# Staging buffers for w3, a later pooled sum of v, and the order of work between the dense layers and the first expert

## The chip, the cores and the metric

The kernel runs on one core of one Trainium2 chip. The metric is the device time of one execution in microseconds (us). The core has five engines that run their own instruction queues in order: TensorE (PE in the profile, its weight loads PEld), VectorE (DVE), ScalarE (ACT), GpSimd (POOL) and SyncE (SP). SyncE computes nothing; it issues transfers, and a transfer that must wait there holds up all those queued behind it. Other engines can issue transfers as well.

## The reference

```
x   = attention(q, k, v)            # 4 x 8 heads, 576 positions, 64 wide; two parts added:
                                    #   pooled by 4 along the sequence (q_d, k_d, v_d = means of 4 rows), repeated 4 times
                                    #   local: |i - j| < 4
x   = ((x @ w1) * (x @ w2)) @ w3 @ w_out       # 2304 rows, 512 -> 1024 -> 1024 -> 512
e   = argmax(x @ w_gate); g = softmax weight of e; o = sigmoid(x @ w_output_gate)[e]
out = g * o * (relu(x @ e_w1[e]) @ e_w2[e])    # each row through its one of 8 experts
```

The weights of the dense layers come as 64-bit floats, and results are kept to nearly 32 bits: each large product is three matmuls, of an upper and a lower half (hi x hi, hi x lo, lo x hi).

## The kernel before

**The first 110 us: weights.** 64-bit weights are loaded as 128x512 tiles of 512 KB, turned into 32-bit floats by three VectorE instructions (lines 138 to 140, `f64_bits`) and split into halves by ScalarE and then VectorE or GpSimd. First come eight tiles of w_out (staging buffers W0 to W7), then sixteen of w3: `f64_load("3", n)` puts tile n into buffer W8 + n % 4, so tile n + 4 is loaded once tile n is converted. The loop over `i` (line 932) converts two of them, and TensorE multiplies them with w_out (`wc_half`), so that later layers use one matrix `wc`. Then w1 and w2 follow, whose halves lie in W0 to W15 as well.

**Attention** is cut into 16 units (two heads each) of five steps: `a_T` (sums of q and k, GpSimd), `a_S1` (scores, exponentials), `a_S2` (normalisation), `a_V1` (transposes), `a_V2` (product with v). They run four deep, as `side`, a few in each turn of the weight loop and later of the dense layers. A unit's v comes twice: `vw` for the local part, and `v4` (the profile's tile v) for the pooled part. `v4` has one buffer; its load is issued at the end of step `a_S1`, and two GpSimd additions at the end of `a_S2` (lines 248 and 249) sum it.

**The dense layers** go over six groups of 384 rows: `g1_step` makes hidden rows, `g2_step` multiplies 128 of them with half of `wc`, copies the result to `yb` and stores it to DRAM (`yd`, and the right half to `yh`) from SyncE. The Tile framework puts the instructions of each engine in an order of its own, by the program's order and a planned timeline, unless lines like `issue_after` fix it.

**From the last group to the first expert** the order of TensorE is written out (`ordered`, lines 997 on): the right halves of the last group, what is left of group 4, the routing (`route_pos`, `route_tok`, `route_rank`, `route_idx`), then the left halves of the last group, tiles 0, 1 and 2. `x_gather` fetches the first expert's rows from DRAM by GpSimd: first their right halves (`yh`), and, after the last left half is stored, the left ones (`yd`). `x_prep` transposes them, in three blocks. `ew_load` and `ew_split` load and split expert weights (512 KB each): (0, 0, i) are the four quarters of the first expert's first matrix, (0, 1, i) those of its second. While the left halves are on their way, TensorE does `ga_part`, the half of the first product that needs only the right halves, for six of eight column tiles f (six PSUM tiles), and `route_gtab` (three matmuls for the gate tables). `route_gates` (lines 653 to 657) makes the gates on VectorE. Then `x_prep` of the left halves, `ga_step` for f = 0 to 7, and `gb_step`, the second product, whose f = 6 and 7 need quarter (0, 1, 3). `behind(rows, load)` holds a load until the gather `rows` has landed.

Of the kernel before, what the change touches and what calls it, by code (L numbers as in the profile page):

```python
# [1 line left out]

# [6 lines left out]
F32 = mybir.dt.float32  # L9
# [4 lines left out]
I64 = mybir.dt.int64  # L14
# [6 lines left out]
P = 128  # L21
B, H, S, D = 4, 8, 576, 64
NT, DM, DF, E = 2304, 512, 1024, 8
KD, KF = DM // P, DF // P
G = 384
NG = NT // G
# [22 lines left out]
def attention_moe_kernel(ctx: ExitStack, tc: tile.TileContext, q, k, vw_in, v4_in, w1, w2, w3, w_out,  # L49
# [15 lines left out]
    def mt(shape, dt, name, tag=None, bufs=None):  # L65
        return main.tile(shape, dt, name=name, tag=tag or name, bufs=bufs)
# [52 lines left out]
    def f64_load(m, n):  # L119
        if m == "o":  # L120
            t = mt([P, 512], I64, "f64w", tag=f"W{n}")
            src = w_out[P * n:P * n + P, :]
        elif m == "3":
            t = mt([P, 512], I64, "f64w", tag=f"W{8 + n % 4}")
            src = w3[n]
        else:
            t = mt([P, 512], I64, "f64", tag=f"W{3 + 4 * m}") if n % 2 and n < 6 else mt([P, 512], I64, "f64", bufs=2)
            src = (w1, w2)[m][n]
        for c in pieces(m, n):
            f64_last[0] = nc.sync.dma_start(out=t[:, c], in_=src[:, c])  # L130
        staged[m, n] = t
# [17 lines left out]
    def at(shape, dt, name, bufs=1):  # L149
        return att.tile(shape, dt, name=name, tag=name, bufs=bufs)  # L150
# [24 lines left out]
            nc.sync.dma_start(out=kz[c, h, 3:3 + S], in_=k[u, c])  # L175

    def a_loadd(u):
        v4 = at([72, 2, 4, 2 * D], F32, "v4")
        nc.sync.dma_start(out=v4.rearrange("p k r n -> p (k r n)"), in_=v4_in[u])
        st[u]["v4"] = v4  # L180

    def a_loadv(u):
        vw = at([P, 6, 2 * D], F32, "vw")
# [50 lines left out]
    def a_S2(u):  # L234
        d = st[u]
        sm, ed = d["sm"], d["ed"]
        su = at([P, 6, 2], F32, "su", bufs=2)
        sd = d["zd"]
        nc.vector.tensor_reduce(out=su, in_=sm, axis=AX.X, op=ALU.add)
        nc.vector.tensor_scalar(su, su, 1e-9, None, op0=ALU.add)  # L240
        nc.vector.reciprocal(su, su)
        nc.gpsimd.tensor_tensor(sm, sm, su.unsqueeze(3).to_broadcast([P, 6, 2, 32]), op=ALU.mult)
        nc.vector.reciprocal(sd, sd)
        nc.gpsimd.tensor_tensor(ed, ed, sd.unsqueeze(2).to_broadcast([96, 3, 144]), op=ALU.mult)
        v4 = d["v4"]
        vd = at([72, 2, 2, D], F32, "vd", bufs=2)
        vt = v4[:, :, 0:2]
        nc.gpsimd.tensor_tensor(vt, vt, v4[:, :, 2:4], op=ALU.add)
        nc.gpsimd.tensor_tensor(vd.rearrange("p k h d -> p k (h d)"), vt[:, :, 0], vt[:, :, 1], op=ALU.add)
        d.update(vd=vd)  # L250

    def a_V1(u):
        d = st[u]
        sm, ed = d["sm"], d["ed"]
        sT = at([P, 12, 32], F32, "sT")
        nc.vector.transpose(sT, sm.rearrange("p b h k -> p (b h) k"))
        for j in range(4):
            r = slice(32 * j, 32 * j + 32)
            nc.scalar.copy(out=bd[r, :, 24 * j:24 * j + 24], in_=sT[r, :, 0:24])
        pt = at([72, 2, 288], F32, "pt")  # L260
        for kb in range(2):
            pv = psa.tile([P, 512], F32, name="at", tag="at")
            with burst():
                for qb in range(3):
                    nc.tensor.transpose(pv[0:72, 96 * qb:96 * qb + 96], ed[:, qb, 72 * kb:72 * kb + 72], ident[0:96, 0:96])  # L265
            nc.scalar.copy(out=pt[:, kb], in_=pv[0:72, 0:288])
        d["pt"] = pt
# [149 lines left out]
    def mm3(ps, whi, wlo, xhi, xlo, first, last):  # L417
        nc.tensor.matmul(ps, whi, xhi, start=first, stop=False)  # L418
        nc.tensor.matmul(ps, whi, xlo, start=False, stop=False)  # L419
        return nc.tensor.matmul(ps, wlo, xhi, start=False, stop=last)  # L420
# [34 lines left out]
    lg = {}  # L455
    yn = [0]

    def g2_step(g, t, hf):
        ps = ps2.tile([P, 512], F32, name="g2", tag="g2")
        n0, n1 = HALF[hf], HALF[hf + 1]  # L460
        for f in range(KF):
            c = slice(P * t, P * t + P)
            mm3(ps[:, 0:HN[hf]], hts[g, f][0][:, c], hts[g, f][1][:, c], wc[:, f, 0, n0:n1], wc[:, f, 1, n0:n1],
                f == 0, f == KF - 1)
        r0 = G * g + P * t
        n = DM // 2
        yn[0] += 1
        y = yb[:, yn[0] % 3, :]
        if hf == 1:
            if t == 0:  # L470
                lg[g] = mt([P, CPG, 2 * E], F32, "lg", bufs=2)
            nc.vector.tensor_copy(lg[g][:, t, :], ps[:, n:n + 2 * E])
            nc.vector.tensor_copy(y, ps[:, 0:n])
        else:
            nc.scalar.copy(out=y, in_=ps[:, 0:n])
        store = nc.sync.dma_start(out=yd[r0:r0 + P, n0:n0 + n], in_=y)
        if hf == 1:
            nc.sync.dma_start(out=yh[r0:r0 + P, :], in_=y)
        return store


    def at_psum():
        if psb is None:
            return psa.tile([P, 512], F32, name="at", tag="at")
        return psb.tile([P, 512], F32, name="tr", tag="tr", bufs=2)

    psb = None
    acc = mt([P, E], F32, "acc")
    tab = mt([P, 3, E, NC], F32, "tab")
    rt = {}  # L490
# [184 lines left out]
    def ordered(fn, *args):  # L675
        with tc.issue_after(pe[0]):
            res = fn(*args)
        pe[0] = next(i for i in reversed(nc.cur_bb.bb.instructions) if i.engine == mybir.EngineType.PE)
        return res
# [67 lines left out]
    def ga_part(r, f, k0, k1, first, last):  # L747
        C = CAPS[r]
        hi, lo = ew[r, 0, f // 2]
        if first:  # L750
            if f < 4 or last:
                gp[f] = psb.tile([P, 512], F32, name="g1", tag="g1", bufs=4)
            else:
                gp[f] = ps2.tile([P, 512], F32, name="g2", tag="g2")
        for kk in range(k0, k1):
            c = slice(256 * kk + P * (f % 2), 256 * kk + P * (f % 2) + P)
            mm3(gp[f][:, 0:C], hi[:, c], lo[:, c], xT[r][0][:, kk, 0:C], xT[r][1][:, kk, 0:C],
                first and kk == k0, last and kk == k1 - 1)
# [248 lines left out]
    early = mt([P, 3, 1024], F32, "early", tag="xr")  # L1007
    for i in range(2):
        ew_load(0, 0, i)
    ordered(g2_step, NG - 1, 0, 0)  # L1010
    rows = x_gather(0, 1)
    behind(rows, ew_load(0, 0, 2))
    behind(rows, ew_load(0, 1, 0, early[:, 0]))
    ew_split(0, 0, 0)
    ordered(g2_step, NG - 1, 1, 0)
    for b in range(NBLK[0] - 1):
        ordered(x_prep, 0, b, KD // 2, KD)
    ew_split(0, 0, 1)
    store = ordered(g2_step, NG - 1, 2, 0)
    with tc.issue_after(store.ins):  # L1020
        ew_load(0, 1, 1, early[:, 1])
    rows = x_gather(0, 0)
    behind(rows, ew_load(0, 0, 3))
    last = ordered(x_prep, 0, NBLK[0] - 1, KD // 2, KD)
    with after(last):
        ew_split(0, 0, 2)
        route_gate(NG - 1)
        rhs = mt([P, CPG, 2 * E * NC], F32R, "rhs", tag="W15")
        for c in range(CPG):
            gate_rhs(NG - 1, c, rhs[:, c])  # L1030
        ew_split(0, 1, 0)
    for f in range(6):
        ordered(ga_part, 0, f, KD // 2, KD, True, False)
    ordered(route_gtab, NG - 1, rhs)
    route_gates()
    with tc.issue_after(rows.ins):
        first = ew_split(0, 1, 1)
    for b in range(NBLK[0]):
        last = ordered(x_prep, 0, b, 0, KD // 2)
    with after(last):  # L1040
        ew_split(0, 0, 3)
    for i in range(2, 4):
        behind(rows, ew_load(0, 1, i, early[:, 2] if i == 2 else None))
    for r in range(E):
        for f in range(KF):
            last = ordered(ga_step, r, f)
            if (r, f) == (1, 0):
                with after(last):
                    overflow_tables()
            if f % 2 == 0:  # L1050
                if r > 0:
                    ew_split(r, 1, f // 2)
                elif f < 4:
                    with after(last):
                        ew_split(r, 1, 2 + f // 2)
                if r + 1 < E:
                    ew_load(r + 1, 0, f // 2)
            if f % 2 == 1 and r > 0 and f // 2 < NBLK[r - 1]:
                ordered(o_step, r - 1, f // 2)
            if f == 4 and r + 1 < E:  # L1060
                with tc.issue_after(first.ins):
                    x_gather(r + 1)
        for dc in range(KD if r + 1 < E else 0):
            ordered(gb_step, r, dc)
            with after(last):
                ew_split(r + 1, 0, dc)
            ew_load(r + 1, 1, dc)
            if dc < NBLK[r + 1]:
                ordered(x_prep, r + 1, dc)
# [64 lines left out]
```

## Time and profile before

| | |
|---|---|
| median of 3 runs | 733.2 us (728.99, 733.2, 734.5) |
| the profiled execution | 731.68 us, span 729.9 us (first to last instruction) |
| busy: TensorE, VectorE, ScalarE, GpSimd | 695.8, 422.8, 286.1, 340.7 us |
| mean granted TensorE clock | 0.992 |

The span is what the trace covers; 1.8 us of the execution lie around it. TensorE is busy for 95% of it.

### The profile page before, as it was taken

What the parts mean: (1) busy time and instruction counts of PE and PEld (TensorE: products, weight loads), DVE (VectorE), ACT (ScalarE), POOL (GpSimd) and SP (SyncE); (2) the same over time, 40 slices, a digit from 0 to 9 for tenths busy, and PEclk for the clock granted to TensorE, in tenths of its full rate; (3) what the DMA queues carried; (4) which work ended last, traced back from release to release, by engine and by line L of the source; (5) the groups of instructions that cost most, each with busy time, mean ns of one, the idle gap of its engine ahead of it and who ended that gap; (6) DMA issues with size and microseconds to landing.
All of it is one profiled execution on the core that took longest, in us unless ns stands there. A gap on an engine that the chain in (4) does not pass through costs nothing.

```text
span 729.9 us, 14702 instructions
## 1 busy us (share of the span) xinstructions
PE 695.8 (95%) x5710; PEld 666.0 (91%) x5711; DVE 422.8 (58%) x884; ACT 286.1 (39%) x664; POOL 340.7 (47%) x339
## 2 busy tenths in 40 slices
PE   5887999999999999999999999989999999999995
PEld 3677989899999999999999999979999999999994
DVE  8997889854545446253242343575776656765830
ACT  3455435563444136135212121345353444544510
POOL 6975567873562157032011020166474655765511
PEclk9999999999999999999999999999999999999998
DMA  8978546363243043111100101665454744545301
GB/s 327 265 251 250 217 124 214 108 196 119 83 126 102 30 109 97 52 40 44 37 30 1 44 1 44 207 246 180 154 175 145 257 159 162 208 169 198 116 25 42
DMA packets 38266, 97.73 MB, mean 134 GB/s; under 512 B 6019, under 2 KB 12931, under 8 KB 38193
## 3 DMA queue, kind: packets, MB, share of 16 engines
q1 hardware_dynamic: 34768, 86.82, 36.5%
q0 software_dynamic: 3424, 9.93, 3.8%
q8 instruction: 46, 0.75, 0.5%
q14 instruction: 28, 0.22, 0.1%
HBM read 84.93 MB, written 12.29 MB: 133 GB/s over the span
## 4 chain that ended last, share of the span: by engine, by line
PE 77%; issue 7%; POOL 5%; DVE 5%; DMA 3%; ACT 1%; SPq 0%; POOLq 0%; DVEq 0%; ACTq 0%
PE g L418 23%; PE g L419 22%; PE g L420 22%; PE at L281 2%; DMA v<-in_v_dram 2%; PE tr L712 1%; PE at L221 1%; PE at L277 1%; DVE cv L139 1%; PE at L209 1%; PE tr L805 1%; DVE cv L138 1%; DVE wf L140 1%; PE at L265 1%; POOL out_dram L795 1%
## 5 line engine op out<-in xcount | busy, mean ns | idle before, releaser
L418 PE MATMUL g<-xh,W 128*128 128x384 f32 x384 | 131.9, 344 | 0.9 <-ACT a L446 0.9
L420 PE MATMUL g<-xh,W 128*128 128x384 f32 x384 | 129.2, 337 | 0.8 <-POOL W L397 0.7
L419 PE MATMUL g<-xl,W 128*128 128x384 f32 x384 | 129.2, 336 | 0.0
L739 DVE TENSOR_TENSOR W<-raw,W 128x1024 fp32r<-128x1024 f32 x32 | 87.7, 2771 | 32.8 <-ACT W L737 23.6
L739 POOL TENSOR_TENSOR W<-raw,W 128x1024 fp32r<-128x1024 f32 x29 | 82.9, 2879 | 36.0 <-ACT W L737 33.0
L418 PE MATMUL g<-xT,W 128*128 128x288 f32 (+6 forms) x256 | 81.5, 318 | 1.0 <-ACT xT L716 1.0
L419 PE MATMUL g<-xT,W 128*128 128x288 f32 (+6 forms) x256 | 79.8, 312 | 0.0
L420 PE MATMUL g<-xT,W 128*128 128x288 f32 (+6 forms) x256 | 79.6, 311 | 0.0
L451 POOL TENSOR_TENSOR h<-a,h 128x384 fp32r<-128x384 f32 x30 | 30.6, 1021 | 101.6 <-ACT h L449 101.6
L418 PEld LDWEIGHTS g<-xh,W 128*128 128x128 f32 x384 | 72.1, 188 | 2.6 <-ACT a L446 1.5
L420 PEld LDWEIGHTS g<-xh,W 128*128 128x128 f32 x384 | 72.1, 188 | 1.9 <-POOL W L397 1.8
L419 PEld LDWEIGHTS g<-xl,W 128*128 128x128 f32 x384 | 72.2, 188 | 0.1
L418 PE MATMUL g<-h,W 128*128 128x288 f32 (+5 forms) x224 | 69.9, 312 | 0.0
L418 PE MATMUL g<-wc,h 128*128 128x272 f32 (+1 forms) x240 | 68.7, 287 | 0.0
L419 PE MATMUL g<-wc,h 128*128 128x272 f32 (+1 forms) x240 | 68.3, 286 | 0.0
L419 PE MATMUL g<-h,W 128*128 128x288 f32 (+5 forms) x224 | 68.0, 304 | 0.0
L420 PE MATMUL g<-h,W 128*128 128x288 f32 (+5 forms) x224 | 68.0, 303 | 0.0
L420 PE MATMUL g<-wc,h 128*128 128x272 f32 (+1 forms) x240 | 67.9, 285 | 0.0
L737 ACT CAST W<-raw 128x1024 fp32r<-128x1024 f32 x61 | 59.8, 1046 | 9.0 <-DMA raw<-in_moe_w_dram 4.9
L447 DVE TENSOR_TENSOR a<-g,a 128x384 f32<-128x384 f32 x48 | 26.6, 554 | 55.6 <-PE g L420 50.3
L765 ACT ACTIVATE h<-g 128x288 fp32r<-128x288 f32 (+6 forms) x64 | 28.0, 437 | 77.1 <-PE g L420 71.5
L795 POOL DMA_INDIRECT out_dram<-orow,b_si x24 | 23.5, 978 | 62.9 <-DVE orow L794 59.3
(257 smaller groups left out, 1702.2 us busy)
## 6 DMA issues: line engine op xcount, KB each, us to landing
raw<-in_moe_w_dram SPq DMA_DIRECT2D x61, 512.0 KB
f64w<-in_moe_w_dram SPq DMA_DIRECT2D x16, 512.0 KB
f<-in_moe_w_dram SPq DMA_DIRECT2D x16, 512.0 KB
vw<-in_vw_dram SPq DMA_DIRECT2D x16, 384.0 KB
kc<-in_k_dram SPq DMA_DIRECT2D x16, 288.0 KB
qT<-in_q_dram SPq DMA_DIRECT2D x16, 288.0 KB
kz<-in_k_dram SPq DMA_DIRECT2D x32, 144.0 KB
v<-in_v_dram SPq DMA_DIRECT2D x16, 288.0 KB
```

The source lines that it names most:

```text
L138: nc.vector.tensor_scalar(c, hi, 3, 0x3FFFFFF8, op0=ALU.logical_shift_left, op1=ALU.bitwise_and)
L139: nc.vector.scalar_tensor_tensor(c, hi, 0xC0000000, c, op0=ALU.bitwise_and, op1=ALU.bitwise_or)
L281: nc.tensor.matmul(xl[c // 3][64 * h:64 * h + 64, 96 * (c % 3):96 * (c % 3) + 96], vw[:, c, D * h:D * h + D], bd[:, 2 * c + h, :], start=T ...
L418: nc.tensor.matmul(ps, whi, xhi, start=first, stop=False)
L419: nc.tensor.matmul(ps, whi, xlo, start=False, stop=False)
L420: return nc.tensor.matmul(ps, wlo, xhi, start=False, stop=last)
L447: nc.vector.tensor_tensor(a, pp[1][:, 0:G], a, op=ALU.mult)
L451: eng.tensor_tensor(lo, a, hi.bitcast(F32), op=ALU.subtract)
L737: nc.scalar.copy(out=hi, in_=t)
L739: ins = eng.tensor_tensor(lo, t, hi.bitcast(F32), op=ALU.subtract)
L765: return nc.scalar.activation(out=t[:, 0, 0:C], in_=ps[:, 0:C], func=AF.Relu), nc.vector.scalar_tensor_tensor(t[:, 1, 0:C], ps[:, 0:C], 0. ...
L795: ins = nc.gpsimd.indirect_dma_start(out=out, out_offset=bass.IndirectOffsetOnAxis(ap=rt["si"][0:n, r, b:b + 1], axis=0), in_=t[0:n], in_o ...
```

## The change

Sixteen w3 tiles rotate through ten staging buffers in place of four (W0, W1, W2, W4, W5, W6 are those of w_out that w1 and w2 don't use for their own staging). `v4` has two buffers, and its two sums move from the end of `a_S2` to the start of `a_V1`, one step later. In the stretch before the first expert: the stores of the last three left halves are issued by ScalarE; the last block's right-half transposes stand in the middle of the last `g2_step` instead of behind it; `ga_part` does seven column tiles, the seventh in one of the two PSUM tiles of the transposes, which then have one while the flag `alone` is set; `route_gtab` moves behind column tile 1 of the first expert, and `route_gates` behind its last one; quarter (0, 0, 3) is loaded with (0, 0, 2), before the left-half gather, and split before the gate work; all four quarters (0, 1, i) are split behind `ga_step` f = 0, 2, 4 and 6, the first two of which were split earlier before, and (0, 1, 1) is loaded after the left-half gather.

```diff
-            t = mt([P, 512], I64, "f64w", tag=f"W{8 + n % 4}")
+            t = mt([P, 512], I64, "f64w", tag=f"W{(8, 9, 10, 11, 0, 1, 2, 4, 5, 6)[n % 10]}")
...
-        v4 = at([72, 2, 4, 2 * D], F32, "v4")
+        v4 = at([72, 2, 4, 2 * D], F32, "v4", bufs=2)
...
-        v4 = d["v4"]
+
+    def a_V1(u):
+        d = st[u]
+        sm, ed, v4 = d["sm"], d["ed"], d["v4"]
         vd = at([72, 2, 2, D], F32, "vd", bufs=2)
         vt = v4[:, :, 0:2]
         nc.gpsimd.tensor_tensor(vt, vt, v4[:, :, 2:4], op=ALU.add)
         nc.gpsimd.tensor_tensor(vd.rearrange("p k h d -> p k (h d)"), vt[:, :, 0], vt[:, :, 1], op=ALU.add)
...
-    def g2_step(g, t, hf):
+    def g2_step(g, t, hf, middle=None, queue=None):
...
+            with tc.issue_after(pe[0]) if middle and f > KF // 2 else nullcontext():
+                end = mm3(ps[:, 0:HN[hf]], hts[g, f][0][:, c], hts[g, f][1][:, c], wc[:, f, 0, n0:n1], wc[:, f, 1, n0:n1],
+                          f == 0, f == KF - 1)
+            if middle and f == KF // 2:
+                pe[0] = end.ins
+                middle()
...
-        store = nc.sync.dma_start(out=yd[r0:r0 + P, n0:n0 + n], in_=y)
+        store = (queue or nc.sync).dma_start(out=yd[r0:r0 + P, n0:n0 + n], in_=y)
...
-        return psb.tile([P, 512], F32, name="tr", tag="tr", bufs=2)
+        tr[0] += 1
+        tag = "tr" if alone[0] or tr[0] % 2 else "tx"
+        return psb.tile([P, 512], F32, name="tr", tag=tag, bufs=1)
...
-            if f < 4 or last:
+            if f == 6 and not last:
+                gp[f] = psb.tile([P, 512], F32, name="tr", tag="tx", bufs=1)
+            elif f < 4 or last:
...
-    ordered(g2_step, NG - 1, 0, 0)
+    ordered(g2_step, NG - 1, 0, 0, None, nc.scalar)
     rows = x_gather(0, 1)
-    behind(rows, ew_load(0, 0, 2))
+    for i in range(2, 4):
+        behind(rows, ew_load(0, 0, i))
     behind(rows, ew_load(0, 1, 0, early[:, 0]))
     ew_split(0, 0, 0)
-    ordered(g2_step, NG - 1, 1, 0)
+    ordered(g2_step, NG - 1, 1, 0, None, nc.scalar)
     for b in range(NBLK[0] - 1):
         ordered(x_prep, 0, b, KD // 2, KD)
     ew_split(0, 0, 1)
-    store = ordered(g2_step, NG - 1, 2, 0)
-    with tc.issue_after(store.ins):
-        ew_load(0, 1, 1, early[:, 1])
+    last = []
+    ordered(g2_step, NG - 1, 2, 0, lambda: last.extend(ordered(x_prep, 0, NBLK[0] - 1, KD // 2, KD)), nc.scalar)
     rows = x_gather(0, 0)
-    behind(rows, ew_load(0, 0, 3))
-    last = ordered(x_prep, 0, NBLK[0] - 1, KD // 2, KD)
     with after(last):
         ew_split(0, 0, 2)
+        ew_split(0, 0, 3)
         route_gate(NG - 1)
         rhs = mt([P, CPG, 2 * E * NC], F32R, "rhs", tag="W15")
         for c in range(CPG):
             gate_rhs(NG - 1, c, rhs[:, c])
-        ew_split(0, 1, 0)
-    for f in range(6):
+    alone[0] = True
+    for f in range(7):
         ordered(ga_part, 0, f, KD // 2, KD, True, False)
-    ordered(route_gtab, NG - 1, rhs)
-    route_gates()
-    with tc.issue_after(rows.ins):
-        first = ew_split(0, 1, 1)
     for b in range(NBLK[0]):
         last = ordered(x_prep, 0, b, 0, KD // 2)
-    with after(last):
-        ew_split(0, 0, 3)
-    for i in range(2, 4):
-        behind(rows, ew_load(0, 1, i, early[:, 2] if i == 2 else None))
+    for i in range(1, 4):
+        behind(rows, ew_load(0, 1, i, early[:, i] if i < 3 else None))
+    first = None
     for r in range(E):
         for f in range(KF):
             last = ordered(ga_step, r, f)
...
-                elif f < 4:
+                else:
                     with after(last):
-                        ew_split(r, 1, 2 + f // 2)
+                        split_ = ew_split(r, 1, f // 2)
+                        first = split_ if f == 2 else first
                 if r + 1 < E:
                     ew_load(r + 1, 0, f // 2)
+            if r == 0 and f == 1:
+                ordered(route_gtab, NG - 1, rhs)
+            if r == 0 and f == KF - 1:
+                alone[0] = False
+                with after(last):
+                    route_gates()
```

## Rows read from the trace of the kernel before

**Rows 1.** The page: busy us of each engine, share of the span, instructions.
```profile
PE 695.8 (95%) x5710; PEld 666.0 (91%) x5711; DVE 422.8 (58%) x884; ACT 286.1 (39%) x664; POOL 340.7 (47%) x339
```
**Rows 2.** Windows: length, busy us by engine (instructions), granted clock, DMA share, GB/s.
```profile
20.00:30.00 10.00, 8.12 (x103) 6.02 (x100) 8.56 (x17) 6.03 (x20) 9.68 (x15) 1.00 1.01 305
30.00:40.00 10.00, 8.47 (x104) 7.50 (x104) 9.97 (x24) 3.44 (x12) 8.18 (x11) 1.00 0.80 231
20.00:69.00 49.00, 40.26 (x511) 35.41 (x508) 43.49 (x91) 25.47 (x84) 37.23 (x51) 1.00 0.87 260
```
**Rows 3.** TensorE's waits, 20 to 150 us: total us, times, longest.
```profile
PE g L418 <- DVE wc L383: 6.5, 4, 3.9
PE at L209 <- DMA kz<-in_k_dram: 1.4, 1, 1.4
```
**Rows 4.** Timelines of SP, POOL, ACT, PE, 53 to 70 us: start, us, instruction, [idle before].
```profile
53.12 0.33 SPq L168 DMA_DIRECT2D kc<-in_k_dram  x1
...
60.19 1.28 POOL L248 TENSOR_TENSOR v<-v 72x512 f32<-72x512 f32 x1 [4.04 <-DMA v<-in_v_dram]
63.41 0.67 POOL L197 TENSOR_TENSOR kc<-kc 128x288 f32<-128x288 f32 x1 [1.07 <-DMA kc<-in_k_dram]
...
65.43 0.52 ACT L227 ACTIVATE sm<-sm 128x384 f32<-128x384 f32 x1 [4.23 <-POOL sm L215]
69.18 0.40 PE L418 MATMUL g<-wo,w3T 128*128 128x272 f32 x1 [3.89 <-DVE wc L383]
```
**Rows 5.** SyncE's waits, 20 to 90 us: total us, times, longest.
```profile
SPq L130 <- DVE wf L140: 10.3, 8, 3.6
SPq L179 <- POOL vd L249: 6.9, 5, 2.3
```
**Rows 6.** GpSimd and TensorE, 92 to 95 us: the last v sum of the stage.
```profile
92.27 1.31 POOL L248 TENSOR_TENSOR v<-v 72x512 f32<-72x512 f32 x1 [2.79 <-DMA v<-in_v_dram]
94.86 0.39 PE L420 MATMUL g<-wo,w3T 128*128 128x256 f32 x1 [0.96 <-POOL w3T L371]
```
**Rows 7.** Window over the first of two stretches of lower clock.
```profile
70.35:73.76 3.41, 3.41 (x17) 3.40 (x16) 1.84 (x4) 1.23 (x4) 2.44 (x4) 0.50 0.59 167
```
**Rows 8.** Timelines of PE, ACT, SP and POOL, 467 to 483 us; window of `ga_part`.
```profile
467.58 0.35 SPq L725 DMA_DIRECT2D raw<-in_moe_w_dram  x1
470.39 0.33 PE L712 MATMUL tr<-ident,xr 96*128 96x96 f32 x2
471.03 0.33 SPq L476 DMA_DIRECT2D yd<-yb  x1
475.19 0.96 POOL L694 DMA_INDIRECT xr<-yd,b_g  x1 [10.21 <-DVE r_gs L574]
476.45 0.95 POOL L694 DMA_INDIRECT xr<-yd,b_g  x1 [0.30 <-issue]
477.37 0.86 PE L599 MATMUL tr<-rhs,rb 128*128 128x288 f32 x3
477.71 0.92 POOL L694 DMA_INDIRECT xr<-yd,b_g  x1 [0.30 <-issue]
479.32 0.41 PE L712 MATMUL tr<-ident,xr 128*128 128x128 f32 x2 [0.85 <-DMA xr<-yd,b_g]
481.57 0.38 PE L712 MATMUL tr<-ident,xr 96*128 96x96 f32 x2 [1.84 <-DVE xT L716]
482.36 0.42 PE L418 MATMUL g<-xT,W 128*128 128x352 f32 x1 [0.41 <-ACT xT L716]
...
471.28:477.37 6.09, 6.09 (x36) 5.88 (x37) 5.29 (x18) 3.37 (x5) 1.88 (x2) 1.00 0.59 195
```
**Rows 9.** Timelines of GpSimd and VectorE, 478 to 482 us.
```profile
478.65 2.35 POOL L739 TENSOR_TENSOR W<-early,W 128x1024 fp32r<-128x1024 f32 x1
478.77 2.41 DVE L655 TENSOR_TENSOR b_gt<-tab 128x144 f32<-128x144 f32 x1
```
**Rows 10.** The page's groups of instructions: ScalarE's casts of expert weights.
```profile
L737 ACT CAST W<-raw 128x1024 fp32r<-128x1024 f32 x61 | 59.8, 1046 | 9.0 <-DMA raw<-in_moe_w_dram 4.9
```

More of the change, by code (lines that the diff above doesn't have):

```diff
@@ L1 @@
-from contextlib import ExitStack, contextmanager
+from contextlib import ExitStack, contextmanager, nullcontext
 import concourse.bass as bass
@@ L177, in a_loadd @@
     def a_loadd(u):
-        v4 = at([72, 2, 4, 2 * D], F32, "v4")
+        v4 = at([72, 2, 4, 2 * D], F32, "v4", bufs=2)
         nc.sync.dma_start(out=v4.rearrange("p k r n -> p (k r n)"), in_=v4_in[u])
-        st[u]["v4"] = v4
+        st.setdefault(u, {})["v4"] = v4
     def a_loadv(u):
@@ L249, in a_S2 @@
         nc.gpsimd.tensor_tensor(vd.rearrange("p k h d -> p k (h d)"), vt[:, :, 0], vt[:, :, 1], op=ALU.add)
[L250 to L254, printed above, removed]
+        d["vd"] = vd
         sT = at([P, 12, 32], F32, "sT")
@@ L462, in g2_step @@
             c = slice(P * t, P * t + P)
-            mm3(ps[:, 0:HN[hf]], hts[g, f][0][:, c], hts[g, f][1][:, c], wc[:, f, 0, n0:n1], wc[:, f, 1, n0:n1],
-                f == 0, f == KF - 1)
+            with tc.issue_after(pe[0]) if middle and f > KF // 2 else nullcontext():
[4 more added lines that the diff above has]
+                middle()
         r0 = G * g + P * t
@@ L484, in at_psum @@
             return psa.tile([P, 512], F32, name="at", tag="at")
-        return psb.tile([P, 512], F32, name="tr", tag="tr", bufs=2)
+        tr[0] += 1
+        tag = "tr" if alone[0] or tr[0] % 2 else "tx"
+        return psb.tile([P, 512], F32, name="tr", tag=tag, bufs=1)
     psb = None
+    tr, alone = [0], [False]
     acc = mt([P, E], F32, "acc")
```

## The prediction

> **What bounds the kernel now.** I read the page first: TensorE is busy for 95% of the span [rows 1], so only its gaps, its slow clock and its work itself can give time back. The change takes no matmul away. Its gaps then show in the windows and the lists of waits: in 20 to 69 us it stands 8.7 of 49 us [rows 2], then for moments up to 143 us, then in the stretch before the first expert, 478 to 483 us [rows 8]. Between 150 and 465 us the list of waits names none, so time saved early is kept, if VectorE keeps up.
>
> In the first region one gap stands out: TensorE waits 3.89 us at 65.3 us. The reader should follow it back [rows 4]. TensorE waits for VectorE's part of `wc_out`, which waits for ScalarE, which had stood 4.23 us at an exponential whose input GpSimd had not made. GpSimd had stood 4.04 us at the addition on v and then 1.07 us for kc, both loads. kc was issued at 53.12 and used at 63.41. The windows say why loads were late: the DMA engines are full in 20 to 30 us (share 1.01, 305 GB/s), only 0.80 busy in 30 to 40, and later loads are slow again; over 20 to 69 us the share is 0.87, at 260 GB/s [rows 2]. SyncE, which issues in order, meanwhile stands 10.3 us for staging tiles to be converted and 6.9 us for the one v4 buffer [rows 5]. So the load path is idle early and crowded late.
>
> In the second region the chain is store, gather, transpose [rows 8]. The last left half is stored at 471.03; the gather starts at 475.19; its blocks are 1.26 us apart; TensorE gets the second block 2.87 us after its issue (479.32 - 476.45). The third transpose then waits 1.84 us for VectorE, whose own instruction at 478.77 took 2.41 us while GpSimd split (0, 1, 1) in 478.65 to 481.00 [rows 9].
>
> After each of the two gaps TensorE runs 3.41 us at a granted clock of 0.50, 1.2 GHz in place of 2.4 [rows 7]: 1.7 us lost each time. The first begins 1.2 us after the 3.89 us gap ends, the second 1.0 us after 482.36.
>
> **The change part by part: the weight stage.** Ten staging buffers let six w3 tiles (six times 512 KB, 3.1 MB) go out before tile 0 of w3 is converted, and the second v4 buffer removes SyncE's wait for the first; v4 is also needed one step later. The idle DMA share of 20 to 69 us is 0.13 x 49 = 6.4 us, enough for 1.7 MB at 260 GB/s [rows 2], which would otherwise stand in front of kc and v. kc would need to come 3.9 us earlier, so the gap can go whole. But removing v's wait alone is worth nothing there: kc's wait at 63.41 would just begin sooner. Both edits are needed, and they come together.
> What can go: the 3.89 us [rows 4], the 1.7 us of clock behind it [rows 7], and 0.96 us at 94.86, which follows from another 2.79 us of GpSimd waiting for v [rows 6]: together 6.6. What is late next: VectorE. It is busy 9.97 of 10 us in 30 to 40 and 43.49 of 49 over the stretch, so at most 5.5 us can be gained there before it is the bound [rows 2]; and TensorE's other waits of this stage are of 1.4 us (kz) and, on `wc`, 6.5 - 3.9 = 2.6 in three [rows 3]. Loads that come out in a new order make other gaps of this size; I give back two of 1.1, 2.2 us. The two additions on v (the first 1.28 us [rows 4]) move, they don't grow; in their new place they stand in front of later GpSimd work of the same length, and cost nothing as long as `a_V2` comes a step later. Stage: -6.6 + 2.2 = **-4.4**, between -8.2 (5.5 + 1.7 + 0.96, VectorE's limit) and the rival below.
>
> **The way to the first expert.** Count from the last left half to the first matmul that needs it, 482.36 before [rows 8].
> - Transposes in the middle of `g2_step`: 0.33 us of TensorE work now stands before the last left half instead of behind it, so its store is 0.33 later. TensorE no longer waits for their copies before `ga_part`, but as it waits for the gather afterwards, nothing is gained by that.
> - The store from ScalarE: SyncE issued it at 471.03, behind a load of 512 KB issued at 467.58 and one more [rows 8]. 475.19 is 4.2 us after issue. The trace has no transfer from ScalarE. Bounds: no gain (the same 4.2), and 1.3 us, if the store takes what the nearest transfer, a gather block, takes from issue to use, 2.87. A loss below nothing I leave out of the middle, and price it as a rival. On ScalarE each of the three issues stands in front of its next copy, 0.33 us as on SyncE, and those copies are due before TensorE needs them. I take 0.7, about the middle. The Trainium skill's page "DMA: Bandwidth & Descriptors", in "Issuing engines are not separate DMA queues", says that transfers from any engine run on the same sixteen DMA engines and that issuing from several saves only the issue time; by that this edit alone is worth nothing, and the whole sum would be 0.7 worse. Its section "Queues, rings and completion order" has each DMA engine alternate between the queues, which would let the store pass the loads.
> - GpSimd no longer splits (0, 1, 1) at 478.65, and `route_gates` is gone from VectorE, so the third block is ready when it lands: 477.71 + 2.87 = 480.58, its transposes 0.79 before the first matmul (482.36 - 481.57), so 481.37; plus 0.33, minus 0.7: **481.0**, 1.36 us earlier. One PSUM tile for three blocks makes each wait until the block before is read out; the blocks come 1.26 us apart, and from a transpose to the next use take 0.79, so I price this at nothing; if the copies take longer than the 1.26, at some 0.3.
> - Work moved across the wait: the seventh half, 6 matmuls of 0.169 (6.09 / 36) = 1.0 us, goes before it, `route_gtab`, 0.86, behind it: -0.15.
> - New wait: quarter (0, 1, 3) is split by GpSimd behind f = 6, after the next expert's gather (three blocks of 1.26), which itself is behind the split of (0, 1, 1). From 481.0: f = 0 to 2 and `route_gtab` end at 484.9, ScalarE's copy (some 0.45) and cast (1.05 [rows 10]) at 486.4, GpSimd's split (2.35 [rows 9]) 488.8, gathers 492.6, split 495.0; `gb_step` wants it about 493.5. TensorE would stand some 1.5 us; if GpSimd's order is the other way, none; if the split takes longer, 2.0. I take 1.0.
> - Quarters (0, 0, 2) and (0, 0, 3) are loaded behind one gather and are due 4 and 6 us after `ga_part` begins; 1 MB at 300 GB/s takes 3.5: hidden.
> - The second slow-clock stretch stays: TensorE still stands about 3 us here (seven halves of 1.0 from about 470.8 end near 477.8).
> Stage: -1.36 - 0.15 + 1.0 = **-0.5**, between -3.8 (the whole 1.3 at the store, -2.0, no new wait, -0.15, no slow clock, -1.7) and +1.2 (no gain at the store, 2.0 of wait: -0.66 - 0.15 + 2.0).
>
> **Sum.** -4.4 - 0.5 = -4.9 against the profiled execution's 731.7: 726.8. The median of the three runs, 733.2, lies 1.5 above it; half of that I add: **727.5**.
>
> **The rivals.**
> - *kc takes v's place.* The extra tiles fill the queue in front of kc as they did before; the long gap and its slow clock stay, only the 0.96 us goes. For it: a DMA share of 0.87 on average and 1.01 in 20 to 30 [rows 2]. Against it: 0.80 in 30 to 40 [rows 2]. -0.96 - 0.5: 731.
> - *Slower: the tiles crowd out the first units of attention.* Between 7 and 21 us six more loads go in front of kz and kc of unit 1, at a time when the DMA engines are full [rows 2]: 3.1 MB at 305 GB/s is 10.3 us. TensorE already waits 1.4 us for that kz [rows 3]. It decides if more than 4.9 us of the 10.3 get through the units to the first split of x, at which the dense layers start. If all do: 731.7 + 10.3 - 4.9 = 737.
> - *All of it goes.* Stage one at VectorE's limit, -8.2, stage two at its best, -3.8: 720.
> - *The new order costs in stage two.* ScalarE's next weight cast is planned ahead of the last copy and store and waits for its load there, a cast of 1.05 [rows 10] in front of the store, and GpSimd's split comes late: 731.7 - 4.4 + 1.2 + 1.05, 729.6. On ScalarE all later casts are queued behind it.
>
> **How the numbers follow.** Forecast 0.46 (own range 724 to 731); kc in v's place 0.18; slower 0.12; all of it 0.14; late in stage two 0.10. The range is 721 to 734: outside lie half of the best case and the slower one, 0.19. One per cent, 7.3 us, is about what a measurement of this kernel can tell from none: faster by more (under 725.9) is the best case and a third of the forecast, 0.14 + 0.16, and 0.02 of the others, 0.32; slower by more (over 740.5) needs more than the whole crowding, 0.06; the rest, 0.62, is within.
>
> **What would show it.** Right: no 4 us wait of GpSimd for v and no 3.89 us gap near 65 us; no stretch at 0.50 near 70 us; DMA share over 0.9 in 30 to 40 us; the first gather block before 475; no 2.4 us VectorE instruction before the first expert; a wait of TensorE for a GpSimd split in the first `gb_step`. Wrong: a long wait for kz or kc between 25 and 45 us, or VectorE waiting for staged tiles; the dense layers starting no earlier; a planned order of ScalarE that puts a cast in front of the last store.

## The result, and the profile after

The changed kernel takes 741.13 us (median of four runs, 739.76 to 744.09) against 733.52 for the kernel before (728.99 to 734.5): ratio 1.0123, 95% interval 1.0098 to 1.0148. The forecast was 727.5, the range 721 to 734. The change makes the kernel slower, and it was forecast to make no difference or a gain.

The profiled execution took 742.3 us, span 740.5, granted clock 0.983: 10.6 us more than the one before. First the page, then the windows of the kernel after (columns as in [rows 2]); the fourth goes from the last product of the last left half to the first product of the second expert, and the last two are stretches of lower clock in it.

```profile
PE 698.7 (94%) x5710; PEld 668.9 (90%) x5711; DVE 423.4 (57%) x884; ACT 286.4 (39%) x664; POOL 342.4 (46%) x339
```
```profile
20.00:30.00 10.00, 6.75 (x92) 5.10 (x92) 8.73 (x18) 6.28 (x19) 9.85 (x15) 1.00 1.03 343
30.00:40.00 10.00, 6.53 (x47) 6.19 (x48) 9.94 (x23) 4.38 (x14) 7.50 (x9) 0.94 1.04 309
20.00:69.00 49.00, 38.98 (x423) 35.74 (x424) 43.97 (x85) 21.82 (x68) 33.93 (x45) 0.93 0.93 287
...
473.41:520.92 47.51, 39.09 (x217) 37.24 (x215) 20.45 (x40) 20.37 (x33) 22.99 (x15) 0.86 0.55 194
482.49:492.73 10.24, 7.58 (x25) 6.42 (x26) 3.69 (x7) 2.92 (x6) 0.92 (x1) 0.50 0.71 260
506.39:509.80 3.41, 3.41 (x15) 3.35 (x14) 0.96 (x2) 1.98 (x3) 3.41 (x2) 0.50 0.66 174
```
The stretch of the kernel before that answers to the fourth of these windows:
```profile
470.27:510.38 40.11, 36.42 (x219) 34.86 (x217) 24.89 (x41) 20.62 (x34) 22.46 (x15) 0.96 0.65 230
```
The two starts lie 3.14 us apart (473.41 - 470.27) and the stretches differ by 7.40 (47.51 - 40.11): together 10.54 of the 10.6. So between these two executions 7.4 us were lost in the first expert and its approach, 3.1 ahead of it. In the later stretch TensorE's idle time rose from 3.69 to 8.42 us, by 4.7; its busy time rose by 2.7, for the same matmuls but two transposes that now stand ahead of it. The granted clock says why: 0.50 for 13.65 us in place of 3.41 [rows 7 shows the like], which loses half of what TensorE works in them. Part of that is the execution and not the kernel: in the profiles of a_w3, a_v4 and a_both (below), whose later stage is that of the kernel before, the first of these stretches is 6.83 us long and not 3.41, and in b_sp, with the later edits, it is 6.83 and not 10.24.

The waits of TensorE in that stretch of the kernel after (us in total, times, longest):
```profile
PE g L419 <- POOL W L745: 3.7, 1, 3.7
PE tr L718 <- DMA xr<-yd,b_g: 2.4, 1, 2.4
PE tr L718 <- DVE xT L722: 1.8, 2, 0.9
```
Before, the stall at the gather was 0.85 us and that at the third transpose 1.84 [rows 8]. The timelines of the kernel after, SP, ACT, POOL and PE in this order, show the approach:
```profile
470.21 0.96 SPq L731 DMA_DIRECT2D raw<-in_moe_w_dram  x2
471.38 0.33 SPq L734 DMA_DIRECT2D early<-in_moe_w_dram  x1
...
474.13 1.05 ACT L743 CAST W<-raw 128x1024 fp32r<-128x1024 f32 x1 [1.18 <-DMA raw<-in_moe_w_dram]
475.65 1.05 ACT L743 CAST W<-raw 128x1024 fp32r<-128x1024 f32 x1 [0.47 <-DMA raw<-in_moe_w_dram]
476.72 0.35 ACT L478 COPY yb<-g 128x256 f32<-128x256 f32 x1
477.11 0.33 ACTq L479 DMA_DIRECT2D yd<-yb  x1
...
479.87 1.12 POOL L700 DMA_INDIRECT xr<-yd,b_g  x1 [12.93 <-DVE r_o L590]
...
482.90 0.66 PE L718 MATMUL tr<-ident,xr 128*128 128x128 f32 x2 [2.44 <-DMA xr<-yd,b_g]
484.48 0.69 PE L718 MATMUL tr<-ident,xr 128*128 128x128 f32 x2 [0.92 <-DVE xT L722]
486.09 0.58 PE L718 MATMUL tr<-ident,xr 96*128 96x96 f32 x2 [0.92 <-DVE xT L722]
487.08 0.66 PE L417 MATMUL g<-xT,W 128*128 128x352 f32 x1 [0.41 <-ACT xT L722]
```
The reader should see the order on ScalarE: two weight casts, each of which waits for its load, stand in front of the last copy and the last store, which goes out 3.70 us after the last left-half product (477.11 - 473.41; before 0.76, 471.03 - 470.27). Behind it, the transposes of the second and third block wait 0.92 us each for the block before to be read out of the one PSUM tile. And the first product of `gb_step` that needs quarter (0, 1, 3) (the expectations call it the first gated product), in the timelines of POOL and PE:
```profile
494.76 2.40 POOL L745 TENSOR_TENSOR W<-early,W 128x1024 fp32r<-128x1024 f32 x1 [11.30 <-ACT W L743]
497.31 1.78 POOL L700 DMA_INDIRECT xr<-yd,b_gi  x1 [0.15 <-issue]
...
501.85 1.62 POOL L700 DMA_INDIRECT xr<-yd,b_gi  x1 [0.30 <-issue]
503.49 7.00 POOL L745 TENSOR_TENSOR W<-raw,W 128x1024 fp32r<-128x1024 f32 x3
505.90 0.43 PE L419 MATMUL g<-h,W 128*128 128x352 f32 x1 [3.72 <-POOL W L745]
```
GpSimd splits (0, 1, 1), issues the second expert's gathers (four, 497.31 to 503.47), and only then splits (0, 1, 3), the first of the three at 503.49. TensorE stands 3.72 us for it and then runs slow from 506.39. In the kernel before, the same subtraction was GpSimd's too, and also behind the four gathers:
```profile
481.16 0.98 POOL L694 DMA_INDIRECT xr<-yd,b_gi  x1 [0.16 <-issue]
...
488.87 2.42 POOL L739 TENSOR_TENSOR W<-raw,W 128x1024 fp32r<-128x1024 f32 x1 [3.01 <-DVE h L765]
```
There it kept nobody waiting, because the split of (0, 1, 1), behind which the gathers are issued, was done at 481.00 [rows 9], ahead of the first expert. The change puts that split behind `ga_step` f = 2, and with it the gathers and the split of (0, 1, 3).

In the weight stage the forecast's signs came out half right. The DMA share in 30 to 40 us is 1.04 (it was 0.80 [rows 2]), yet TensorE is busy 1.3 us less in 20 to 69. Its waits in 20 to 150 us, SyncE's in 20 to 90, and the timelines of SP, POOL, ACT and PE about the longest gap, all after:
```profile
PE g L417 <- DVE wc L382: 7.5, 4, 3.3
...
SPq L168 <- POOL kd L198: 7.3, 3, 3.6
SPq L179 <- POOL vd L252: 3.9, 3, 2.4
```
```profile
34.69 3.87 SPq L130 DMA_DIRECT2D f64w<-in_moe_w_dram  x3
40.14 0.33 SPq L179 DMA_DIRECT2D v<-in_v_dram  x1
...
49.75 1.27 POOL L251 TENSOR_TENSOR v<-v 72x512 f32<-72x512 f32 x1 [3.88 <-DMA v<-in_v_dram]
50.99 0.83 POOL L215 TENSOR_TENSOR sm<-sm,mx 128x384 f32<-128x384 f32 x1
51.85 0.52 ACT L227 ACTIVATE sm<-sm 128x384 f32<-128x384 f32 x1 [3.49 <-POOL sm L215]
...
55.07 0.39 PE L417 MATMUL g<-wo,w3T 128*128 128x272 f32 x1 [3.30 <-DVE wc L382]
```
This is the chain of [rows 4] again, 14 us earlier: v late on GpSimd, behind it the next unit's scores, ScalarE's exponential, VectorE's part of `wc`, TensorE. SyncE stands less for the v4 buffer (3.9 us, 6.9 before [rows 5]) and 7.3 us for a kc buffer.

### The profile page after: what moved, and what is told of

Its sections match the earlier page's. It is cut to its first block, busy times and chain, and to the rows that moved or that the text cites. A ratio compares the mean times of both kernels' runs of the same rounds, so it can differ in the third digit from the quotient of the medians.

```text
span 740.5 us, 14684 instructions
## 1 busy us (share of the span) xinstructions
PE 698.7 (94%) x5710; PEld 668.9 (90%) x5711; DVE 423.4 (57%) x884; ACT 286.4 (39%) x664; POOL 342.4 (46%) x339
## 4 chain that ended last, share of the span: by engine, by line
PE 70%; DMA 12%; issue 7%; POOL 6%; DVE 4%; ACT 0%; SPq 0%; POOLq 0%; DVEq 0%
PE g L417 21%; PE g L419 21%; PE g L418 20%; DMA v<-in_v_dram 4%; DMA f64w<-in_moe_w_dram 3%; PE at L280 2%; PE tr L718 1%; PE at L221 1%; PE at L209 1%; PE tr L813 1%; POOL xr L700 1%; POOL W L745 1%; PE at L276 1%; POOL out_dram L803 1%; DMA vw<-in_vw_dram 1%
## 5 line engine op out<-in xcount | busy, mean ns | idle before, releaser
L745 DVE TENSOR_TENSOR W<-raw,W 128x1024 fp32r<-128x1024 f32 x32 | 85.2, 2692 | 32.1 <-ACT W L743 25.5
L417 PE MATMUL g<-xT,W 128*128 128x288 f32 (+6 forms) x252 | 80.5, 320 | 0.4 <-ACT xT L722 0.4
L418 PE MATMUL g<-xT,W 128*128 128x288 f32 (+6 forms) x252 | 78.5, 312 | 0.0
L419 PE MATMUL g<-xT,W 128*128 128x288 f32 (+6 forms) x252 | 78.4, 311 | 0.0
```

Of the source, the lines that this page charges most:

```text
L745: ins = eng.tensor_tensor(lo, t, hi.bitcast(F32), op=ALU.subtract)
```

## The experiments

All ratios are to the kernel before, run beside it on the same chip, with 95% intervals.

**The two halves.** The weight stage's edits one by one and together, without the later edits, and the later edits alone:
```diff
 a_w3:   + the ten tags for w3            a_v4:   + v4 bufs=2, sums of v in a_V1
 a_both: + both                           b_only: + everything else of the change
```
*Ten tiles alone.* 

> The kernel before with the ten staging buffers for w3 alone. Theory 1 (crowding: the six extra tiles go in front of kc and kz of the next attention units) expects the weight stage 1 to 3 us later, so 1.001 to 1.004 times before, with a wait of GpSimd for kc near 40 us. Theory 2 (the later sums and early loads of v4 cost) expects it as fast as before or up to 4 us faster.

*v4 alone.* 

> The kernel before with the two v4 buffers and the sums of v in a_V1 alone. Theory 1 expects a gain of 1 to 5 us, with GpSimd's waits for v gone and no 3.9 us gap of TensorE near 65 us. Theory 2 expects 1 to 2 us more than before, with GpSimd still waiting for v.

*Both.* 

> The kernel before with both edits of the weight stage and nothing else. From the two traces TensorE is 1.4 us later at its 1500th instruction and 2.0 us later at its 4000th, so both theories expect 1.002 to 1.003 times before, about 2 us. If the edits of the later stage were needed for that delay, it would be the same as before.

*Later edits alone.* 

> The changed kernel with the weight stage as before. TensorE lost 8.6 us between its 4050th and 4200th instruction, so the theory that the two stages simply add expects 8 to 9 us more than before, 1.011 to 1.012. If the stages interact (planned order, clock), anything from 5 to 11 us.

Measured: ten tiles 732.07 us, 0.9972 (0.9948 to 0.9996); v4 733.44, 1.0005 (0.9982 to 1.0027); both 733.31, 1.0007 (0.9984 to 1.0030); later edits 739.5, 1.0084 (1.0053 to 1.0116). The loss is in the later edits, and the weight stage gives nothing as it stands.

**The later edits, one cause at a time**, each on b_only:
```diff
 b_sp     -  stores of the last left halves on nc.scalar       + on nc.sync
 b_cast   -  with after(last):                                 + with after(last), tc.issue_after(store.ins):
 b_split  -  eng = ... or (r == 0 and m == 0)                  + ... or (r == 0 and (m == 0 or i == 3))   # VectorE
 b_tr2    -  seven upper halves, one PSUM tile                 + six upper halves, two PSUM tiles
 b_order  -  x_gather(1) ahead of the split of (0,1,3)         + behind it; both stay on GpSimd
```


> The changed later stage alone, with quarter (0,1,3) split by VectorE in place of GpSimd. If the split behind the next expert's gather is what TensorE waits 3.7 us for in the first gb_step, that wait goes and the slow clock behind it (1.7): 5 to 5.5 us less, 1.001 to 1.003 times before. If VectorE is then late itself, 2 us less.

Measured: 732.54 us, 0.9991 (0.9958 to 1.0023): 6.8 us below b_only by the two ratios (0.0093 of 733), give or take some 3.3, as they are from two chips. TensorE's wait for the split in b_only, and after it its waits of the same stretch in b_split, with no line for a split:
```profile
PE g L420 <- POOL W L746: 3.7, 1, 3.7
```
```profile
PE tr L719 <- DMA xr<-yd,b_g: 2.4, 1, 2.4
PE tr L719 <- DVE xT L723: 1.8, 2, 0.9
```
One engine for one subtraction is all that differs, and nearly the whole loss is gone.

> The later-stage edits alone, with one change of order on GpSimd: the next expert's four gathers go behind the split of (0,1,3), not ahead of it; GpSimd still makes that split. Theory (it is the place in GpSimd's queue that costs, not the engine): the split ends near 28 us after the last left-half product, before the first gated product wants it at 29, so the 3.7 us wait goes and with it a slow-clock stretch of 1.7 to 3.4; the gathers come some 4 us later, and a wait of 0 to 2 us for their first block may show in its place. 733 to 736.5, ratio 1.000 to 1.004. Rival (GpSimd is too slow for that split, or its weight or cast comes late): the wait stays at 3 us or more, ratio 1.007 to 1.010.

Measured: 735.88 us, 1.0072 (1.0046 to 1.0098). The wait for the split is gone, as the first theory had it, but its size was wrong, as the ratio is not told from b_only's: the same stretch has a new wait, for the second expert's gather (`b_gi`), followed by a slow stretch:
```profile
PE tr L719 <- DMA xr<-yd,b_gi: 2.3, 1, 2.3
PE tr L719 <- DMA xr<-yd,b_g: 2.3, 1, 2.3
```
GpSimd has a split of 2.4 us and four gathers to do for work that TensorE reaches at nearly the same time; in these two orders, whichever goes second is waited for.

> The changed later stage alone, with ScalarE's casts of quarters (0,0,2) and (0,0,3) and the gate exponentials ordered behind its last copy and store. If those casts, which wait for their loads, hold the last store, it leaves 2.5 to 3 us earlier, the gather too, and the time is 3 to 5 us under the changed later stage alone, 1.003 to 1.006 times before. If the loads on the DMA engines hold the store anyway, no change, 1.008.

> The changed later stage alone (weight stage as before), with the last three stores issued by SyncE again. If the place of the copy in ScalarE's order is what delays the gather, the issuer does not matter: within 1 us of the changed later stage alone (6 to 8 us over before). If a queue of ScalarE's own lets the store pass the weight loads, 1 to 2 us slower than that.

Measured: b_cast 738.33, 1.0070 (1.0044 to 1.0097); b_sp 737.8, 1.0073 (1.0045 to 1.0101): neither is told from b_only. Both ran on b_split's chip, and by the means b_split is 5.2 us below b_cast and 5.3 below b_sp (+- 2.2). Store and gather in the timelines of b_only, b_sp and b_cast:
```profile
475.63 0.33 ACTq L480 DMA_DIRECT2D yd<-yb  x1
478.16 0.97 POOL L701 DMA_INDIRECT xr<-yd,b_g  x1 [12.21 <-DVE r_o L591]
```
```profile
473.89 0.33 SPq L480 DMA_DIRECT2D yd<-yb  x1
476.42 0.99 POOL L701 DMA_INDIRECT xr<-yd,b_g  x1 [13.18 <-DVE r_o L591]
```
```profile
469.69 0.33 ACTq L480 DMA_DIRECT2D yd<-yb  x1
475.06 1.13 POOL L701 DMA_INDIRECT xr<-yd,b_g  x1 [12.39 <-DVE r_o L591]
```
From store to gather it is 2.53 us on either queue (478.16 - 475.63, 476.42 - 473.89): with no load under way, ScalarE's queue gained nothing. It gained nothing behind loads either: with two loads issued within the 4 us before the store, it is 3.90 to 4.75 us from ScalarE (fix_ld, fix_ld_2, w3_fix_ld, w3_fix_ld_2, fix_ld_both, fix_ld_both_2) and was 4.16 from SyncE before [rows 8]. That agrees with the Trainium skill, "DMA: Bandwidth & Descriptors", section "Issuing engines are not separate DMA queues". With the casts behind it, b_cast's store goes out 0.72 us after the last product and not 4.16, but then takes 5.37 us: of the 3.4 us won at the issue, 0.6 is left at the gather. In the traces the store's last packet ends 1.33 us after its issue in b_only and b_sp, 4.03 after it in b_cast, and the gather follows 1.2 to 1.4 us later. The brackets name VectorE's r_o, but the gather does not need it: in fix_ld (below) it starts at 475.39, and that line of r_o runs at 476.91.

> The changed later stage alone, with six upper halves and two PSUM tiles for the transposes, as before. If the one PSUM tile costs what the two waits of 0.92 us for VectorE show, the first matmul of the left halves comes 1 to 1.8 us earlier, but 1.0 us of work is behind it again: 0 to 1 us less in all. If the seventh half hides anything, slower by 0.5 to 1.

Measured: 736.36 us, 1.0041 (1.0012 to 1.0071). TensorE's waits there:
```profile
PE tr L719 <- DMA xr<-yd,b_g: 4.8, 3, 3.6
PE g L420 <- POOL W L746: 2.1, 1, 2.1
```
```profile
479.21 0.66 PE L719 MATMUL tr<-ident,xr 128*128 128x128 f32 x2 [0.83 <-DMA xr<-yd,b_g]
480.30 0.55 PE L719 MATMUL tr<-ident,xr 96*128 96x96 f32 x2 [0.43 <-DMA xr<-yd,b_g]
```
The two waits of 0.92 us for the one PSUM tile are gone, but waits of 0.83 and 0.43 us for the gather stand in their place. The wait for the split is 1.6 us shorter than in b_only: beside b_sp, whose first slow stretch is as long, and counted from the first left-half product, TensorE comes to the split 0.9 us later, with one more upper half to do, and GpSimd is done 0.8 sooner. So this run's time says what the pair costs together, not the tile alone.

**Corrections, to see whether the causes add up.** after_split is the whole change with VectorE's split; b_cast_split is b_only with b_split's and b_cast's lines; fix_ld adds to that:
```diff
-    behind(rows, ew_load(0, 1, 0, early[:, 0]))     # ahead of the last store
...
-    for i in range(1, 4):
+    for i in range(4):                              # all four behind the left-half gather
         behind(rows, ew_load(0, 1, i, early[:, i] if i < 3 else None))
```


> The whole change, with one step taken back: the upper half of quarter (0,1,3) is split by VectorE again, not by GpSimd. Theory (the split standing on GpSimd behind the next expert's four gathers is most of the loss): the 3.7 us wait of the first gated expert goes, and one slow-clock stretch with it, so 6 to 9 us below the change, 732 to 735, ratio to before 0.999 to 1.003. Rival (the weight stage and the late store carry an equal share in the whole change): 737 to 739, ratio 1.005 to 1.008.

Measured: 734.51, 1.0017 (0.9993 to 1.0041): below the change by 6.6 us in the medians, 7.8 by the ratios (0.0106 of 733).

> The later-stage edits alone, with the split of (0,1,3) by VectorE and the two casts and the gate exponentials ordered behind the last copy and store on ScalarE. Theory (the casts cost about half a microsecond of the left-half gather, the rest of its lateness being the weight loads): the gather ends 6.1 us after the last left-half product, 0.3 to 0.6 us sooner than with the split alone, and the time is 730 to 732.5, ratio 0.996 to 1.000. Rival (the casts' lateness counts in full once the split is out of the way): 2 to 3 us below the split alone, 729.5 to 730.5.

> As the kernel with both corrections, and the weight of (0,1,0) is loaded behind the left-half gather, so that 1 MB of weight loads and not 1.5 MB stands ahead of the last store. Theory (the loads hold the store's completion): the gather ends 4.9 to 5.2 us after the last left-half product in place of 6.1, the first left-half product of the first expert starts as much sooner, and the time is 1 us lower, 729 to 731.5. Rival (the store's completion is long for another reason, its issue from ScalarE): the gather still ends at 6.1 and the time is that of the kernel with both corrections, or up to 1 us more if (0,1,0) comes late.

Measured: b_cast_split 731.94, 0.9980 (0.9956 to 1.0004); fix_ld 730.0, 0.9958 (0.9937 to 0.9979). The timelines of ACT and POOL in fix_ld:
```profile
471.49 0.33 ACTq L480 DMA_DIRECT2D yd<-yb  x1
475.39 1.20 POOL L701 DMA_INDIRECT xr<-yd,b_g  x1 [10.13 <-DMA yd<-yb]
```
3.90 us from store to gather with two loads ahead (1 MB), 5.37 in b_cast with three. The first theory held in this pair, and by the means fix_ld is 1.9 +- 1.7 us below b_cast_split, on one chip. But what the third load costs by itself is not separated: fix_ld_v4, with the same two loads ahead of its store, took 5.49 (store at 468.36, gather at 473.85), and in it as in b_cast the trace shows 0.26 MB on ScalarE's queue behind the store's issue, two stores of 128 KB, so that the store before was still to be moved.

**The weight stage in company with the corrected later stage**: fix_ld with ten tiles (w3_fix_ld), with v4 (fix_ld_v4), and with both.

> As the run before, with ten staging tiles for w3 as well. Theory (that edit gives up to 0.3 per cent by itself, and the stages are far apart, so the gains add): 727 to 730, ratio 0.993 to 0.997. Rival (the weight stage's timing varies from execution to execution by as much as the edit gives): no difference from the run before, 729 to 731.5.

> The kernel with the three corrections of the later stage (split by VectorE, casts behind the store, (0,1,0) loaded behind the gather), with the two tiles for the values and their later sums, without the ten staging tiles. Theory (these edits are worth nothing, as by themselves): ratio to before 0.994 to 0.998, that of the three corrections alone. Rival (in company with the later edits the weight stage loses 2 to 3 us, as the last left half in both executions of the whole weight stage stood 2 to 3 us later than elsewhere, and the values are the part that does it): 0.998 to 1.001.

> The whole change with the three corrections of the later stage: both edits of the weight stage are in. Theory (both together are worth nothing, as by themselves): ratio to before 0.994 to 0.998. Rival (the two edits together lose 2 to 3 us): 0.997 to 1.001; if the kernel with the values alone stays at 0.994 to 0.998, it takes both, and the crowding of the loads is its cause.

Measured: 728.79, 0.9942 (0.9921 to 0.9963), beside fix_ld's run; on another chip fix_ld_v4 730.28, 0.9993 (0.9970 to 1.0017), and fix_ld_both 731.51, 0.9997 (0.9972 to 1.0023). As the chips' own times of before differ, three were run once more on one chip:

> The three corrections of the later stage with the weight stage of before, once more, beside the two that follow on one chip. Theory (the weight stage's edits are worth nothing): the ratio of this kernel and that of the two others agree within 0.002. Rival (the values' two tiles cost 2 us in company with the later edits, as the call of before it suggests): this kernel and that with ten tiles alone stay at 0.994 to 0.997, and that with both edits is 0.003 or more above them.

> As that, with the ten tiles for w3 alone. Theory (worth nothing): within 0.002 of the run before it. Rival (a gain of 0.2 to 0.3 per cent, as this edit gave by itself): 0.992 to 0.995.

> As that, with both edits of the weight stage. Theory (worth nothing): within 0.002 of the three corrections alone. Rival (2 us lost): 0.003 or more above them, 0.998 to 1.001.

Measured: fix_ld_2 730.18, 0.9952 (0.9929 to 0.9974); w3_fix_ld_2 729.48, 0.9945 (0.9920 to 0.9971); fix_ld_both_2 731.56, 0.9977 (0.9950 to 1.0004). The three overlap. Taken with a_w3 and a_both, which also shared a chip, v4 on top of the ten tiles costs 1.64 +- 1.67 and 1.76 +- 1.82 us (differences of the means of 10 and of 12 runs), 1.7 +- 1.2 weighted together; neither pair alone is told from nothing. TensorE's waits in 20 to 150 us show where; this line in a_w3, a_both, w3_fix_ld_2, fix_ld_both_2:
```profile
PE g L418 <- DVE wc L383: 0.6, 2, 0.5
```
```profile
PE g L417 <- DVE wc L382: 5.1, 4, 2.0
```
```profile
PE g L418 <- DVE wc L383: 1.2, 1, 1.2
```
```profile
PE g L417 <- DVE wc L382: 6.2, 4, 2.8
```
With ten tiles alone the waits for `wc` all but go (in w3_fix_ld there is none); with v4 on top of them they are back. By itself v4 does not raise them: 3.2 us in a_v4, 1.9 in fix_ld_v4. (The line has two numbers, as the edits shift it.) In ten executions with the weight stage of before they are 3.0 (b_split) to 6.5 us [rows 3].

The best kernel of all is the later stage with its three corrections and ten tiles for w3, 0.6% below before; the tiles' own share of it is not told from nothing in that company.

## Why the prediction was wrong

The forecast had -0.5 us for the later edits and -4.4 for the weight stage. By themselves they measured +6.2 (b_only, 0.0084 of 733) and +0.5 (a_both). The whole change, +9.0 by its ratio, is 2.3 more than the two, within their intervals.

**The step that failed most is "New wait", in the way to the first expert.** Its mechanism was right: GpSimd splits (0, 1, 3) behind the second expert's gathers, and TensorE waits for it. Its size was 1.0 us and it measured 3.72, and what hangs on it was left out. Counted from the first left-half product (487.08), the split of (0, 1, 1) ended after 10.1 us and not 7.8, as its cast waits for f = 2, whose products ran in the slow stretch. Then come four gathers, not three, in 6.3 us (497.16 to 503.49) against 3.8; the trace of the kernel before has four too. TensorE was only 2.6 us later than forecast. And behind the wait comes another slow stretch, 1.7 us, which the same prediction had priced after the two gaps that it read. "If the split takes longer, 2.0" was no upper bound. The wait and its slow stretch are 5.4 us together; b_split is 5.2 and 5.3 below b_cast and b_sp beside it and 6.8 +- 3.3 below b_only, and after_split 6.6 to 7.8 below the whole change, so they account for most of the loss, and nothing more is shown.

**The rival "the new order costs in stage two" was the right sign for the wrong price.** A cast did go in front of the last store, two in fact, and the store was 2.6 us later than the forecast's 0.76 + 0.33. But at the gather only 0.6 us of it counts (b_cast). That the loads hold an early store is shown by its packets (last one after 4.03 us and not 1.33); no run took all loads away. The rival priced 1.05 for the cast and 1.2 for the rest, and set both against a gain of 4.4 that did not come.

**"I price this at nothing", the one PSUM tile**, was small, but not nothing. The estimate compared 0.79 (transpose to next use) with 1.26 (gather cadence). The tile is free only after ScalarE's copy and VectorE's subtraction have both read it, 1.6 us a block (484.48 - 482.90), so the profile names the read-out, and not the gather, as what ended both waits of 0.92 us. They are not its price, though, as two tiles wait for the gather there. From the issue of the third gather to its transposes it takes 2.74 us in b_tr2 (480.30 - 477.56) and 3.0 to 3.5 in the runs on b_only that have one tile: 0.3 to 0.7 us. Before it took 3.86 (481.57 - 477.71), with the wait of 1.84 in it, so a part of what freeing VectorE of `route_gates` gave was kept.

**"I take 0.7" for the store from ScalarE** should have been the lower bound, nothing: 2.53 us on either queue with no load under way, and no gain behind loads; the store did not pass them. The Trainium skill's sentence on the issue time, which the prediction set beside it, was the better one.

**The weight stage, "-4.4", came out as nothing by itself** (a_both 1.0007) **and about +1.2 us beside the corrections** (fix_ld_both_2 against fix_ld_2, within +- 1.7). Two steps failed. One execution's gap was taken as the kernel's: 3.89 us at 65 us in the profile shown, but 1.4 in b_split, which runs the same weight stage; the slow stretch at 70 us [rows 7] is absent there, and one of 6.83 us stands at 29 us in its place. And "both edits are needed" was the reverse of what the runs showed: the ten tiles alone all but remove the waits for `wc`, and beside them the second v4 buffer brings them back. Little time came of it, 0.9972 in a_w3; TensorE's waits for GpSimd's splits of w3 grew to 1.9 us there, from 1.0. GpSimd's waits for v did not shrink, though SyncE's wait for v4 did; the loads that went ahead, three of w3 at 34.69, stand in front of v. Why the values' edits bring the chain back while the ten tiles alone, with v as late, do not, was not tried further and stays open. "Crowding", the slower rival with 10.3 us of loads in front, is not what was seen: a_w3 has the extra loads and is not slower than before.

**The 3.1 us ahead of the last left half** in the profile after are more than fix_ld_both_2 and fix_ld_both show (471.24 and 470.25 for the same product, 470.27 before); after_split stands at 473.21. With the differences of the medians within their intervals, this part is not settled. **What held:** the DMA share over 0.9 in 30 to 40 us, no 2.4 us instruction of VectorE before the first expert, a wait for a GpSimd split in the first `gb_step`, the second slow stretch staying.

## What to carry to other kernels

Before a step is moved behind others on an in-order engine, add up all that is queued there, against the moment at which the next engine wants each of them; if two are wanted at once, neither order of the two may help, and one has to start earlier, as in the kernel before, or go to another engine, as in b_split. Where a gap is followed by a slow clock, price both. And take a wait on a crowded load path from several executions before building a gain on it.

## What the runs showed of the hardware

The stretches at a granted clock of 0.50 in the later stage were 3.41, 6.83 or 10.24 us long, and not always the same for the same edits (3.41 before, 6.83 in a_w3). In the kernel after they stood at the waits of 2.44 and 3.72 us. The one of 10.24 began 0.4 us before the first product behind the wait of 2.44 (482.49 against 482.90), lasted through the two waits of 0.92 between the transposes and ended 5.65 us after the dense run of products began (492.73 - 487.08).

The same store of 128 KB took 2.53 us until the gather could start when no load had been issued for 5.9 us or more (b_only, b_sp), 3.90 to 4.75 behind two loads of 512 KB issued within the 4 us before it, and 5.37 and 5.65 behind three (b_cast, b_cast_split); in fix_ld_v4 it was 5.49 behind two, with the store before it still to be moved.
